# Six PSUM banks of scores: three sides of two banks in place of two sides of three

## The chip, the cores and the metric

The kernel runs on one core of a Trainium2 chip. A core has four engines that matter here: TensorE (PE in the profile) multiplies matrices and writes into PSUM, ScalarE (ACT) applies functions such as the exponential, VectorE (DVE) and GpSimd (POOL) do element-wise arithmetic. PSUM holds eight banks of 128 partitions x 512 float32 values; the kernel uses six of them for attention scores. The metric is the device time in microseconds. Before the change it was 778.63 us, the median of three runs (777.14 to 778.92).

## The reference: what is computed

```
g = sigmoid((x * gate_w).sum(-1))
q, k, v = split(x @ wqkv)                       # 32 heads of width 16, 2048 rows
a = softmax(q k^T / 4) v, joined over heads, @ wo
h = gelu(layernorm(x) @ w1); hs = shifted(h) @ w2; x1 = x + hs
b = x1 + gelu(layernorm(x1) @ w3) @ w4          # 512 -> 1792 -> 512
out = g * a + (1 - g) * b
```

The two halves read the same x (2048 x 512, bfloat16). The attention has 32 x 2048 x 2048 = 134 million scores, and each needs an exponential; that is most of the work outside TensorE.

## The kernel before

**Tiles.** The scores are made in blocks of 128 keys x 512 queries. A unit is four heads with one chunk of 512 queries; there are 32 units, each of 16 key tiles x 4 heads = 64 blocks, 2048 blocks in all. A score block (`score`, L749 to L756) is one matmul with only 32 rows of the array in use (a head's 16 values beside zeros), so blocks of different heads j lie in different row groups and run side by side.

**Two ways to the exponential.** Most blocks are read from PSUM by ScalarE, which writes the exponential as bfloat16 into a tile `pt` (`expo`, L1076). The others go to VectorE: it adds a constant and converts to int16 (`dump` in `whole`, L959), which gives the bits of a bfloat16 that is roughly the exponential. Four such blocks, one key tile for all four heads, make a quad; four further copies of the quad with other constants added (`shifted`, L1000 on VectorE, L998 on GpSimd) are made from it. TensorE sums all five copies in the product with v, and their errors cancel. So a block on ScalarE needs one product with v, and a block on VectorE needs five (`attend`, L1089).

**Slots and sides.** The first 34 slots (`EARLY`) have two banks each. After them six banks are used as two sides of three. Slot k uses side k % 2 (`stage`, L738 to L747). Either all three banks are ScalarE's and it reads 1536 elements per partition at once, or the slot also holds a block for VectorE (`dsc`; the rule WIDE is 1 in every unit), and ScalarE reads 1024 and VectorE 512. A slot of two kinds divides the side into two tiles, in a pool that is opened anew whenever the kind changes. The side is free again when both readers are done: `score_ready` (L716 to L736) waits for the exponential of slot k - 2 and for its dump. `lone_slot` gives a whole side to VectorE around the gelu stages.

**Order.** The order of all instructions is written out by a planner that runs while the kernel is built: four queues (pe, act, vector, pool) with estimated costs (MM, TURN, PE_OUT, ACT_OUT and the costs given to `post`), and it always takes the option that can begin first. TensorE's options are a score turn (`scores`), products with v (`attend`), steps of the projections (`job_run`), the last steps, and a `fill`, a multiplication by zero that keeps TensorE running. `wants_whole` decides whether a score turn carries blocks for VectorE: VectorE's queued work must be under DLIM, a room for the quad must be free, and fewer than CHAINS quads begun; it looks for a key tile that the unit hasn't reached, at most MAXD blocks to a unit. RULES holds such values for each of the 31 later units.

**Other work.** Projections and the MLP go through one more bank (`gen`), from which VectorE copies. The gelus sit in five places; each loads ScalarE's other table, applies the gelu in place to tiles that VectorE has copied, and then reads score sides that TensorE has filled with `g2T` or `hT` columns (`gelu_slot`, `expo_gelu`, L1053 and L1056): two slots of three tiles of 512 in each of the last four places. The last unit's last twelve blocks are cut into three ranges of queries (`split`, `end_slot`), so that the final sums can begin range by range.

Of the kernel before, what the change touches and what calls it, by code (L numbers as in the profile page):

```python
# [32 lines left out]
def kernel(  # L33
# [14 lines left out]
    P = 128  # L48
# [8 lines left out]
    PTB = 6  # L57
# [65 lines left out]
    idle = ptpool.tile([P, 3 * CH], BF16, tag="pt", name="idle")  # L123
# [39 lines left out]
    USUAL = {"WIDE": 1, "NEED": 36, "AHEAD": 8, "HURRY": 8, "DLIM": 0.9, "MANY": 2, "PTS": 4, "CHAINS": 4, "MAXD": 20}  # L163
    RULES = {1: {"MANY": 8, "NEED": 32, "WIDE": 1, "AHEAD": 16, "MAXD": 20, "PTS": 6, "CHAINS": 2, "HURRY": 14, "DLIM": 1.2}, 2: {"NEED": 24, "DLIM": 1.5, "HURRY": 24, "CHAINS": 2, "WIDE": 1, "PTS": 4, "AHEAD": 32, "MANY": 6, "MAXD": 16}, 3: {"WIDE": 1, "NEED": 30, "AHEAD": 20, "HURRY": 4, "DLIM": 1.2, "MANY": 8, "PTS": 5, "CHAINS": 4, "MAXD": 20}, 4: {"WIDE": 1, "NEED": 24, "AHEAD": 10, "HURRY": 0, "DLIM": 1.2, "MANY": 8, "PTS": 6, "CHAINS": 6, "MAXD": 20}, 5: {"WIDE": 1, "NEED": 22, "AHEAD": 16, "HURRY": 18, "DLIM": 2.1, "MANY": 8, "PTS": 6, "CHAINS": 3, "MAXD": 16}, 6: {"PTS": 4, "AHEAD": 6, "WIDE": 1, "DLIM": 2.5, "CHAINS": 3, "HURRY": 24, "MANY": 5, "MAXD": 16, "NEED": 34}, 7: {"WIDE": 1, "NEED": 36, "AHEAD": 24, "HURRY": 4, "DLIM": 1.8, "MANY": 6, "PTS": 5, "CHAINS": 4, "MAXD": 16}, 8: {"WIDE": 1, "NEED": 32, "AHEAD": 32, "HURRY": 14, "DLIM": 0.9, "MANY": 3, "PTS": 3, "CHAINS": 5, "MAXD": 12}, 9: {"DLIM": 1.2, "CHAINS": 2, "MANY": 2, "NEED": 26, "AHEAD": 4, "PTS": 4, "WIDE": 1, "HURRY": 4}, 10: {"MANY": 5, "PTS": 5, "HURRY": 24, "MAXD": 20, "AHEAD": 20, "CHAINS": 2, "NEED": 26, "DLIM": 0.9}, 11: {"WIDE": 1, "NEED": 40, "AHEAD": 8, "HURRY": 14, "DLIM": 1.2, "MANY": 5, "PTS": 6, "CHAINS": 3, "MAXD": 12}, 12: {"WIDE": 1, "NEED": 22, "AHEAD": 4, "HURRY": 24, "DLIM": 1.8, "MANY": 2, "PTS": 5, "CHAINS": 5, "MAXD": 16}, 13: {"WIDE": 1, "NEED": 26, "AHEAD": 12, "HURRY": 8, "DLIM": 0.9, "MANY": 6, "PTS": 6, "CHAINS": 6, "MAXD": 16}, 14: {"WIDE": 1, "CHAINS": 3, "HURRY": 8, "MANY": 6, "NEED": 40, "AHEAD": 32, "PTS": 3, "MAXD": 20, "DLIM": 1.8}, 15: {"DLIM": 2.1, "MAXD": 20, "PTS": 6, "CHAINS": 3, "NEED": 30, "HURRY": 24, "WIDE": 1, "MANY": 5, "AHEAD": 16}, 16: {"CHAINS": 3, "PTS": 4, "AHEAD": 16, "DLIM": 1.8, "HURRY": 4, "NEED": 36, "MANY": 4, "MAXD": 16}, 17: {"MAXD": 16, "DLIM": 0.9, "HURRY": 14, "NEED": 22, "PTS": 5, "WIDE": 1, "CHAINS": 2, "MANY": 4}, 18: {"NEED": 24, "AHEAD": 12, "MAXD": 16, "MANY": 5, "DLIM": 2.5, "CHAINS": 2, "HURRY": 4, "PTS": 6, "WIDE": 1}, 19: {"AHEAD": 8, "MAXD": 20, "DLIM": 1.2, "NEED": 26, "CHAINS": 6, "PTS": 3, "HURRY": 14, "MANY": 5}, 20: {"CHAINS": 2, "MAXD": 12, "WIDE": 1, "MANY": 4, "PTS": 3, "NEED": 30, "AHEAD": 20, "DLIM": 1.2, "HURRY": 24}, 21: {"MANY": 6, "NEED": 40, "CHAINS": 5, "WIDE": 1, "HURRY": 14, "DLIM": 2.1, "AHEAD": 12, "PTS": 3, "MAXD": 16}, 22: {"MANY": 5, "DLIM": 2.1, "AHEAD": 20, "WIDE": 1, "NEED": 40, "CHAINS": 4, "HURRY": 14, "PTS": 5, "MAXD": 16}, 23: {"MANY": 5, "NEED": 24, "DLIM": 2.1, "HURRY": 8, "AHEAD": 32, "WIDE": 1, "PTS": 6}, 24: {"MAXD": 16, "NEED": 28, "AHEAD": 16, "DLIM": 1.2, "MANY": 8, "PTS": 3, "WIDE": 1, "CHAINS": 3, "HURRY": 0}, 25: {"DLIM": 2.1, "PTS": 5, "NEED": 26, "WIDE": 1, "MAXD": 16, "HURRY": 14, "CHAINS": 2, "MANY": 5, "AHEAD": 8}, 26: {"WIDE": 1, "NEED": 28, "AHEAD": 10, "HURRY": 14, "DLIM": 1.8, "MANY": 3, "PTS": 3, "CHAINS": 5, "MAXD": 16}, 27: {"WIDE": 1, "NEED": 30, "AHEAD": 10, "HURRY": 0, "DLIM": 2.5, "MANY": 4, "PTS": 5, "CHAINS": 3, "MAXD": 12}, 28: {"NEED": 36, "PTS": 6, "WIDE": 1, "MAXD": 20, "DLIM": 1.8, "CHAINS": 5, "MANY": 4, "AHEAD": 6, "HURRY": 24}, 29: {"WIDE": 1, "NEED": 30, "AHEAD": 4, "HURRY": 24, "DLIM": 1.5, "MANY": 5, "PTS": 6, "CHAINS": 3, "MAXD": 16}, 30: {"WIDE": 1, "NEED": 26, "AHEAD": 24, "HURRY": 0, "DLIM": 1.5, "MANY": 4, "PTS": 5, "CHAINS": 2, "MAXD": 20}, 31: {"WIDE": 1, "NEED": 24, "AHEAD": 4, "HURRY": 24, "DLIM": 1.2, "MANY": 8, "PTS": 4, "CHAINS": 2, "MAXD": 12}}
    MM = 0.214
    TURN = 0.104
# [7 lines left out]
    VLIM = 2.0  # L174
    LASTNEED = 40
# [3 lines left out]
    LOOK = 0.1  # L179
# [3 lines left out]
    HOLD = (0.15, 0.5)  # L183
    MARGIN = 0.3
    CREDIT = 0.5
    LATER = 0.55
    GELU, WTWO = 1.0, 1.6
    MOST = 16.0
# [4 lines left out]
    SLACK = 0.25  # L193
# [4 lines left out]
    TANH = 3.0  # L198
    WINDOW = 3.4
    LOW = 0.45  # L200
    PINCH = 0.2
# [3 lines left out]
    state = {"n": 0, "gen": 0, "young": True, "mm": 0, "sp": 0.0, "before": True, "after": False, "aside": 0.0, "kind": "", "t": 0.0, "piece": 0.0,  # L205
# [273 lines left out]
    def mlp():  # L479
# [28 lines left out]
        for c in range(NC_):  # L508
            if c < NC_ - 1:
                norm(1, c + 1)  # L510
            g2T = pools["g"].tile([P, FT, CH], BF16, tag="g", name="g2T")
            for m in range(APART):
                yield from before_gelu(w3, m, res[0], g2T[:, m, :], ("z", c, m), all_at(("xnT", 1, c, KT - 1)))
            yield from gelu_all(("g", c), [g2T[:, m:m + 4, :] for m in range(0, APART, 4)],
                                all_at(*[("z", c, m) for m in range(APART)]), w3, res[0],
                                [(range(m, m + 3), g2T[:, m:m + 3, :]) for m in range(APART, FT, 3)])
            if c < NC_ - 1:
                res = []
                yield from norm_T(1, c + 1, res)
            for t in range(4 * c, 4 * c + 4):  # L520
                yield from w4_tile(g2T, w4, c, t)
# [133 lines left out]
    accs, stages, pts, old = {}, {}, {}, {}  # L655
    room = deque(epool.tile([P, 4, CH], I16, name=f"quad{i}")[:] for i in range(7))
    lone, undumped = set(), {}
    scored, dumped, done_exp, users, pt_free = {}, {}, {}, {}, {}
    banksets = [ExitStack(), ExitStack()]
    ctx.callback(lambda: [b.close() for b in banksets])  # L660
    kinds = [None, None]
    next_slot = {"score": 0, "exp": 0}
    group = {}

    def upcoming(count):
# [3 lines left out]
        while len(found) < count and n < len(units):  # L669
# [3 lines left out]
            if (m // 4, m % 4) not in taken[n]:  # L673
                found.append((n, m))
# [9 lines left out]
    def wants_whole(blocks, now, alone=0):  # L684
# [4 lines left out]
        most = alone or rule("WIDE")  # L689
        if quad["open"] is not None:  # L690
            n, kt, rest = quad["open"]
            most = min(most, len(rest))
            heads = [m % 4 for _, m in blocks[:3 - most]]
            fit = [j for j in rest if j not in heads]
            if len(fit) >= most or k - quad["last"] > 2 or alone:
                return n, kt, (fit + [j for j in rest if j in heads])[:most]
            return None
        heads = [m % 4 for _, m in blocks[:3 - most]]
# [17 lines left out]
    def score_ready(k):  # L716

        found = upcoming(1)
        if not found and not gelus and not ends:
            return None  # L720
        t = 0.0
        for n, m in () if gelus else upcoming(2 if k < EARLY else 3):
            c, u = units[n]
            for key in (("q", c, u // 2), ("k", u // 2, m // 4 * P // CH)):
                if key not in at:
                    return None
                t = max(t, at[key])
        if k >= 2:
            if k - 2 not in done_exp or dumped.get(k - 2, 0.0) is None:
                return None  # L730
            t = max(t, done_exp[k - 2] + 0.005, dumped.get(k - 2, 0.0) - 0.12)
        if k == EARLY:
            if k - 1 not in done_exp or banks[1] is None or banks[2] is None or state["bank"] and current["job"]:
                return None
            t = max(t, banks[1], banks[2])
        return t + 0.03  # L736

    def stage(k, kind):  # L738

        side = k % 2  # L740
        if kinds[side] != kind:
            banksets[side].close()
            kinds[side] = kind
            old[side] = banksets[side].enter_context(tc.tile_pool(
                name=f"psS{k}", bufs=1, space=bass.MemoryType.PSUM, side=("left", "right")[side], reuse_waits="tile"))
        st = old[side].tile([P, (3 - kind) * CH], F32, tag="stage", name="stage")
        return st, old[side].tile([P, kind * CH], F32, tag="dsc", name="dsc") if kind else None  # L747
# [10 lines left out]
    def gelu_slot(start):  # L758
        k = len(slots)
        item = turn[k] = gelus.popleft()  # L760
        _, _, _, w, rhs, ms, _, _ = item
        stages[k], _ = stage(k, 0)
        slots.append([])
        state["slot"] = len(slots)
        state["mm"] = 0
        for i, m in enumerate(ms):
            for kt in range(KT):
                strips(stages[k][:, i * CH:(i + 1) * CH], lhsT=w[:, kt, m * P:(m + 1) * P], rhs=rhs[:, kt, :],
                                 start=(kt == 0), stop=(kt == KT - 1))
        free["pe"] = start + (TURN if state["kind"] not in NARROW else 0.0) + len(ms) * KT * MM  # L770
        state["kind"] = "full"
        works(free["pe"] - len(ms) * KT * MM, free["pe"])
# [762 lines left out]
```

## Time and profile before

| | |
|---|---|
| median of three runs | 778.63 us |
| profiled execution | 777.81 us |
| its span, first to last instruction | 776.0 us |
| TensorE busy, share | 748.3 us, 96% |
| ScalarE busy, share | 759.2 us, 98% |
| VectorE busy, share | 717.1 us, 92% |
| GpSimd busy, share | 248.8 us, 32% |
| granted TensorE clock, mean | 1.000 |

A group's row gives its line, engine and operation, what is written from what, the shape, the count, then busy time and mean duration in ns, then the idle time of the engine just before these instructions and what ended it. Instructions of one engine overlap a little at their ends, so a mean duration is longer than the distance from one start to the next.

### The profile page before, as it was taken

What the parts mean: (1) busy time and instruction counts of PE and PEld (TensorE: products, weight loads), DVE (VectorE), ACT (ScalarE), POOL (GpSimd) and SP (SyncE); (2) the same over time, 40 slices, a digit from 0 to 9 for tenths busy, and PEclk for the clock granted to TensorE, in tenths of its full rate; (3) what the DMA queues carried; (4) which work ended last, traced back from release to release, by engine and by line L of the source; (5) the groups of instructions that cost most, each with busy time, mean ns of one, the idle gap of its engine ahead of it and who ended that gap; (6) DMA issues with size and microseconds to landing.
All of it is one profiled execution on the core that took longest, in us unless ns stands there. A gap on an engine that the chain in (4) does not pass through costs nothing.

```text
span 776.0 us, 23911 instructions
## 1 busy us (share of the span) xinstructions
PE 748.3 (96%) x10127; PEld 247.8 (32%) x10128; DVE 717.1 (92%) x1231; ACT 759.2 (98%) x730; POOL 248.8 (32%) x187
## 2 busy tenths in 40 slices
PE   8999999999999999899999999999999999999997
PEld 4334323333333233232223223323332223232233
DVE  5798999999999999999999999999998899989894
ACT  6999999999999999999999999999999999999996
POOL 3221433442313414234451334123224333311420
PEclk9999999999999999999999999999999999999999
DMA  9600012111130006002000013000020000000110
GB/s 198 199 24 18 16 47 64 33 32 42 18 37 19 19 18 125 20 16 46 20 17 22 20 33 45 17 11 14 19 53 21 16 19 26 20 29 6 33 32 31
DMA packets 52308, 29.05 MB, mean 37 GB/s; under 512 B 36713, under 2 KB 47721, under 8 KB 52201
## 3 DMA queue, kind: packets, MB, share of 16 engines
q1 hardware_dynamic: 51240, 27.00, 15.0%
q8 instruction: 79, 1.29, 0.7%
q10 hardware_dynamic: 960, 0.52, 0.2%
q14 instruction: 29, 0.23, 0.1%
HBM read 17.17 MB, written 2.35 MB: 25 GB/s over the span
## 4 chain that ended last, share of the span: by engine, by line
ACT 56%; PE 22%; issue 16%; DVE 5%; DMA 1%; POOL 1%; DVEq 0%; ACTq 0%; POOLq 0%; SPq 0%
ACT pt L1076 51%; PE acc L1089 8%; PE stage L754 7%; PE ps L271 2%; ACT g2T L1053 1%; PE ps_y L271 1%; DVE quad L959 1%; PE ps_o L271 1%; ACT g2T L1056 1%; DVE quad L1000 1%; ACT hT L1053 1%; DMA bcs<-rec_d 1%; POOL oT L1201 1%; ACT L1053 1%; PE warm L1335 0%
## 5 line engine op out<-in xcount | busy, mean ns | idle before, releaser
L1076 ACT ACTIVATE pt<-stage 128x1024 bf16<-128x1024 f32 (+1 forms) x686 | 709.3, 1220 | 4.5 <-PE dsc L754 2.1
L754 PE MATMUL stage<-qT,kT 32*128 32x512 bf16 (+1 forms) x1604 | 271.3, 379 | 18.0 <-ACT pt L1076 12.6
L959 DVE TENSOR_SCALAR quad<-dsc 128x512 int16<-128x512 f32 x346 | 230.6, 685 | 14.1 <-PE dsc L754 12.0
L998 POOL TENSOR_SCALAR quad<-quad 128x2048 int16<-128x2048 int16 x68 | 129.4, 1903 | 260.5 <-DVE quad L1000 146.4
L754 PE MATMUL dsc<-qT,kT 32*128 32x512 bf16 x468 | 179.9, 384 | 0.0
L754 PEld LDWEIGHTS <-kT 32*128 32x128 bf16 x2072 | 83.2, 91 | 284.0 <-issue 247.6
L1089 PE MATMUL acc<-pt,vp 128*17 128x512 bf16 (+3 forms) x1576 | 148.5, 379 | 2.5 <-DVE accsb L1171 1.8
L1000 DVE TENSOR_SCALAR quad<-quad 128x2048 int16<-128x2048 int16 x212 | 147.7, 710 | 1.3 <-PE acc L1089 1.2
L1089 PE MATMUL acc<-quad,vp 128*17 128x512 bf16 x1696 | 144.9, 381 | 0.1
L1089 PEld LDWEIGHTS <-vp 128*17 128x17 bf16 (+1 forms) x4056 | 83.1, 89 | 133.2 <-issue 97.2
L271 PE MATMUL ps<-w,g2T 128*32 128x512 bf16 x896 | 69.3, 382 | 0.0
L1201 POOL TENSOR_TENSOR oT<-accsb,bcs 128x512 bf16<-128x512 f32 x29 | 37.0, 1277 | 84.9 <-DVE quad L1000 60.1
L998 POOL TENSOR_SCALAR more<-more 128x2048 int16<-128x2048 int16 x17 | 32.3, 1897 | 80.8 <-DVE more L1000 33.1
L271 PE MATMUL ps_y<-xnT,w 128*32 128x512 bf16 x704 | 56.3, 383 | 1.0 <-DVE accsb L1171 0.8
L959 DVE TENSOR_SCALAR more<-dsc 128x512 int16<-128x512 f32 x69 | 45.9, 683 | 1.1 <-PE dsc L754 1.0
L998 POOL TENSOR_SCALAR xT<-xT 128x2048 int16<-128x2048 int16 x14 | 26.9, 1919 | 50.9 <-DVE quad L1000 44.4
L1089 PE MATMUL acc<-more,vp 128*17 128x512 bf16 x420 | 39.7, 380 | 0.0
L271 PEld LDWEIGHTS <-w 128*32 128x32 bf16 x1152 | 28.8, 95 | 33.0 <-issue 16.3
L959 DVE TENSOR_SCALAR xT<-dsc 128x512 int16<-128x512 f32 x53 | 35.2, 683 | 1.8 <-PE dsc L754 1.4
L1089 PE MATMUL acc<-xT,vp 128*17 128x512 bf16 x364 | 34.8, 381 | 0.0
L271 PE MATMUL acc<-wq,zero 128*32 128x512 bf16 x324 | 30.0, 383 | 0.0
L1000 DVE TENSOR_SCALAR more<-quad 128x2048 int16<-128x2048 int16 x39 | 27.8, 719 | 0.0
(120 smaller groups left out, 592.7 us busy)
## 6 DMA issues: line engine op xcount, KB each, us to landing
bcs<-rec_d SPq DMA_DIRECT2D x31, 256.0 KB
w<-in_B_w_dram SPq DMA_DIRECT2D x2, 1792.0 KB
out_dram<-ot SPq DMA_DIRECT2D x15, 128.0 KB
x_sb<-in_A_x_dram SPq DMA_DIRECT2D x14, 128.0 KB
oT<-oT SPq DMA_DIRECT2D x112, 16.0 KB
w<-in_B_w_dram SPq DMA_DIRECT2D x2, 512.0 KB
wkv<-in_A_wqkv_dram SPq DMA_DIRECT2D x1, 512.0 KB
wo_all<-in_A_wo_dram SPq DMA_DIRECT2D x8, 64.0 KB
```

The source lines that it names most:

```text
L271: nc.tensor.matmul(out[j:j + 32, :], lhsT=lhsT[:, j:j + 32], rhs=rhs, tile_position=(0, j), **kwargs)
L754: nc.tensor.matmul(out, lhsT=kT[G][32 * j:32 * j + 32, cc, o:o + P], rhs=qTs[(c, G)][32 * j:32 * j + 32, a, lo:hi], start=True, stop=True, ...
L959: nc.vector.tensor_scalar(out=bits[:, r:r + wide, :], in0=dsc.rearrange("p (a c) -> p a c", c=CH), scalar1=SHIFT, scalar2=LOWEST, op0=ALU. ...
L998: behind(nc.gpsimd.tensor_scalar(out=tiles[to], in0=tiles[base], scalar1=1.0, scalar2=shift, op0=ALU.mult, op1=ALU.add))
L1000: fast["ins"] = nc.vector.tensor_scalar(out=tiles[to], in0=tiles[base], scalar1=shift, scalar2=None, op0=ALU.add)
L1053: nc.scalar.activation(out=part, in_=part, func=ACT.Gelu_apprx_tanh)
L1056: nc.scalar.activation(out=dst, in_=stages.pop(k)[:, 0:len(ms) * CH].rearrange("p (a c) -> p a c", c=CH), func=ACT.Gelu_apprx_tanh)
L1076: nc.scalar.activation(out=pt[:, 0:w], in_=stages.pop(k)[:, 0:w], func=ACT.Exp, scale=LN2 / 128.0)
L1089: nc.tensor.matmul(accs[n][32 * j:32 * j + M, lo:hi], lhsT=lhsT, rhs=p, start=(kt == 0), stop=(kt == NT - 1), skip_group_check=True, tile_ ...
L1201: behind(nc.gpsimd.tensor_tensor(out=oT, in0=tiles["accsb"][:], in1=tiles["bcs"][:], op=ALU.mult))
```

## The change

The six banks become three pools of one tile each, two banks wide (`tri`), opened once. `sides` holds the time from which each is free, or None while it is used. ScalarE's slots always have two blocks, and VectorE's fetches always two blocks from a side of their own. `plan` decides when a score turn is made and for how many sides: if a second side will be free before ScalarE is due, the turn waits for both and fills two sides, four blocks, with two for ScalarE and either two for VectorE or two more for ScalarE; else it fills one. `order` lets the heads of a key tile be taken as 2, 3, 0, 1, so that the four blocks lie in four row groups. `alone` is a new TensorE option: a turn with two blocks for VectorE only, when VectorE has little queued. It takes the place of `lone_slot`.

Around it: `pt` tiles hold two blocks in place of three, and there are nine in place of six; the gelu slots take two tiles (three slots in each of the last four places instead of two); the last ranges are read in seven slots in place of four; the last step's PSUM tiles come from the same three sides; the planner's estimates MM and TURN are 0.002 lower; and RULES, USUAL and a dozen constants have new values. WIDE stays in the rules and isn't read any more. The core of the diff:

```diff
-    PTB = 6
+    PTB = 9
...
-                                [(range(m, m + 3), g2T[:, m:m + 3, :]) for m in range(APART, FT, 3)])
+                                [(range(m, m + 2), g2T[:, m:m + 2, :]) for m in range(APART, FT, 2)])
...
-        most = alone or rule("WIDE")
+        most = alone or 2
...
-        if k >= 2:
-            if k - 2 not in done_exp or dumped.get(k - 2, 0.0) is None:
-                return None
-            t = max(t, done_exp[k - 2] + 0.005, dumped.get(k - 2, 0.0) - 0.12)
...
+    def plan():
+
+        free_at = frees()
+        if gelus or ends:
+            return (free_at[0][0] + 0.03, 1, 0.0) if free_at else None
+        if not upcoming(1):
+            return None
+        t = keys_ready(2)
+        if t is None or not free_at:
+            return None
+        runs = [lasts(k) for k in pending()]
+        due_by = free["act"] + sum(runs) - ACT_OUT - TURN - 0.05
+        latest = due_by + PAIRW
+        first = max(t, free_at[0][0])
+        if len(free_at) > 1:
+            if max(t, free_at[1][0]) <= latest:
+                return max(t, free_at[1][0]) + 0.03, 2, due_by
+        elif runs and free["act"] + runs[0] + 0.115 <= latest:
+            return None
+        return first + 0.03, 1, due_by
...
+    def side_for(k):
+        side = frees()[0][1]
+        sides[side] = None
+        if k is not None:
+            side_of[k] = side
+        return side, tri[side].tile([P, 2 * CH], F32, tag="stage", name="stage")
...
+    def scores(start, count):
+        if gelus:
+            return gelu_slot(start)
+        if ends:
+            return end_slot(start)
+        begin = start + (TURN if state["kind"] != "score" else 0.0)
+        rows = [0, 0, 0, 0]
+        k = len(slots)
+        blocks = following_blocks()
...
+        mine = wants_whole(blocks, start) if count == 2 else None
+        put(side_for(k)[1], k, blocks, rows)
+        scored[k] = begin + (max(rows) - 1) * MM + ACT_OUT
+        if mine:
+            put_whole(mine, begin, rows)
+        elif count == 2 and not ends and (keys_ready(4) or 1e9) <= start:
+            blocks = following_blocks()
+            if blocks:
+                k = len(slots)
+                put(side_for(k)[1], k, blocks, rows)
+                scored[k] = begin + (max(rows) - 1) * MM + ACT_OUT
+        done_scores(begin, rows)
+
+    def put_whole(mine, begin, rows):
+        n, kt, js = mine
+        taken[n].update((kt, i) for i in range(4))
+        side, dsc = side_for(None)
+        for i, j in enumerate(js):
+            rows[j] += 1
+            score(dsc[:, i * CH:(i + 1) * CH], n, 4 * kt + j)
+        whole(side, dsc[:, 0:len(js) * CH], n, kt, js, begin + (max(rows) - 1) * MM + PE_OUT)
+
+    def alone_ready(f):
+
+        free_at = frees()
+        if state["young"] or state["ending"] or ends or not free_at:
+            return None
+        mlp = gelus or turn and max(turn) >= next_slot["exp"]
+        if not mlp and (len(pending()) < 2 or not SOLO) or gelus and len(free_at) < 2:
+            return None
+        t = max(f, free_at[0][0] + 0.03)
+        work = free["vector"] - t + sum(x[2] for x in queue["vector"] if not callable(x[4]) and x[4] < t + 1.0)
+        return t if work < (GLIM if mlp else SOLO) and wants_whole([], t, 2) else None
...
         def dump(end):
             nc.vector.tensor_scalar(out=bits[:, r:r + wide, :], in0=dsc.rearrange("p (a c) -> p a c", c=CH), scalar1=SHIFT, scalar2=LOWEST,
                                     op0=ALU.add, op1=ALU.max)
-            undumped[k] -= 1
-            if not undumped[k]:
-                dumped[k] = end
+            sides[k] = end - 0.12
...
-            pt = ptpool.tile([P, 3 * CH], BF16, tag="pt", name="pt")
+            pt = ptpool.tile([P, 2 * CH], BF16, tag="pt", name="pt")
...
         done_exp[k] = free["act"] + 0.11
+        if k in side_of:
+            sides[side_of[k]] = done_exp[k] + 0.005
```

More of the change, by code (lines that the diff above doesn't have):

```diff
@@ L167 @@
+    MM = 0.212
+    TURN = 0.102
     NARROW = ("full", "attend")
@@ L734, in score_ready, with frees, pending, lasts @@
                 return None
-            t = max(t, banks[1], banks[2])
+            t = max(t, banks[1], banks[2], done_exp[k - 1] + 0.005)
         return t + 0.03
[L738 to L747, printed above, removed]
+    def frees():
+        return sorted((t, s) for s, t in enumerate(sides) if t is not None)
+    def pending():
+        return range(next_slot["exp"], len(slots))
+    def lasts(k):
+        if k in turn:
+            return 0.05 + len(turn[k][5]) * CH / 1200 + sum(0.1 + p.free_size() / 1200 for p in turn[k][1])
+        return 0.051 + len(slots[k]) * cut.get(k, CH) / 1200
+    def plan():
+        free_at = frees()
+        if gelus or ends:
+            return (free_at[0][0] + 0.03, 1, 0.0) if free_at else None
+        if not upcoming(1):
+            return None
+        t = keys_ready(2)
+        if t is None or not free_at:
[10 more added lines that the diff above has]
+        return first + 0.03, 1, due_by
     def score(out, n, m, lo=0, hi=CH):
@@ L756, in score, with put @@
                          start=True, stop=True, tile_position=(32 * j, 0))
[L758 to L772, printed above, removed]
[L773 to L803 removed]
+    def put(st, k, blocks, rows):
         stages[k] = st
[L805 to L806 removed]
         for i, (n, m) in enumerate(blocks):
@@ new lines, in following_blocks, with gelu_slot @@
+    def following_blocks():
+        blocks = upcoming(2)
+        if place["n"] == len(units) - 1:
+            blocks = blocks[:max(0, remaining(place["n"]) - SPLIT - 4)]
+        return blocks
+    def side_for(k):
[4 more added lines that the diff above has]
+        return side, tri[side].tile([P, 2 * CH], F32, tag="stage", name="stage")
+    def gelu_slot(start):
+        k = len(slots)
+        item = turn[k] = gelus.popleft()
+        w, rhs, ms = item[3:6]
+        stages[k] = side_for(k)[1]
+        slots.append([])
+        state["slot"] = len(slots)
+        state["mm"] = 0
+        for i, m in enumerate(ms):
+            for kt in range(KT):
+                strips(stages[k][:, i * CH:(i + 1) * CH], lhsT=w[:, kt, m * P:(m + 1) * P], rhs=rhs[:, kt, :],
+                                 start=(kt == 0), stop=(kt == KT - 1))
+        free["pe"] = start + (TURN if state["kind"] not in NARROW else 0.0) + len(ms) * KT * MM
+        state["kind"] = "full"
+        works(free["pe"] - len(ms) * KT * MM, free["pe"])
+        scored[k] = free["pe"] - MM + ACT_OUT
```

231 lines of the change are left out of this document (100 added, 131 removed).

## The prediction

> **What bounds the kernel now.** I read the page first, then the table of windows, then ScalarE's groups by form, then the waits.
>
> ```profile
> span 776.0 us, 23911 instructions
> ...
> PE 748.3 (96%) x10127; PEld 247.8 (32%) x10128; DVE 717.1 (92%) x1231; ACT 759.2 (98%) x730; POOL 248.8 (32%) x187
> ...
> ACT 56%; PE 22%; issue 16%; DVE 5%; DMA 1%; POOL 1%; DVEq 0%; ACTq 0%; POOLq 0%; SPq 0%
> ...
> L1076 ACT ACTIVATE pt<-stage 128x1024 bf16<-128x1024 f32 (+1 forms) x686 | 709.3, 1220 | 4.5 <-PE dsc L754 2.1
> ...
> L271 PE MATMUL acc<-wq,zero 128*32 128x512 bf16 x324 | 30.0, 383 | 0.0
> ```
>
> ScalarE is busy 98% of the span and holds 56% of the chain that ended last. TensorE's 96% is softer: 30.0 us of it are multiplications by zero that the planner puts in to keep it running (the last row). By stage (the columns are the stretch, its length, then busy time and count of PE, PEld, DVE, ACT and POOL, the clock and the DMA):
>
> ```profile
> 0.00:40.00 40.00, 37.77 (x523) 15.97 (x527) 26.41 (x69) 33.68 (x38) 11.20 (x44) 1.00 0.79 195
> 40.00:740.00 700.00, 679.27 (x9192) 219.99 (x9196) 666.01 (x1122) 696.61 (x667) 230.67 (x139) 1.00 0.13 29
> 740.00:776.10 36.10, 31.23 (x420) 11.89 (x413) 24.65 (x42) 28.92 (x27) 6.96 (x4) 0.99 0.10 33
> ```
>
> From 40 to 740 us ScalarE lacks 3.4 us of 700. There is no idle time to win: only less work on ScalarE shortens this kernel, and that means handing score blocks to VectorE, which in the same stretch has 34.0 us idle (700 - 666.0). The start and the end are not touched by the change except in the order of the last slots. So the question is how much ScalarE's reads cost in their new size, and how many blocks VectorE can take over.
>
> **ScalarE: the price of a read.** The forms of its exponential, and a long run of each by the chain in order of time (start, length, what):
>
> ```profile
> L1076 ACT ACTIVATE pt<-stage 128x1024 bf16<-128x1024 f32 x504 | 477.3, 1106 | 4.0 <-PE dsc L754 2.1 <-PE stage L754 1.4
> L1076 ACT ACTIVATE pt<-stage 128x1536 bf16<-128x1536 f32 x181 | 255.1, 1539 | 0.5 <-PE stage L754 0.4
> ...
> L1076 ACT ACTIVATE pt<-stage 128x512 bf16<-128x512 f32 x1 | 0.9, 862 | 0.0
> ...
> 39.40 6.29 ACT pt L1076 x7
> ...
> 570.89 2.68 ACT g2T L1056 x2
> ```
>
> Seven reads of 1024 in 6.29 us are 0.90 us each; two of 1536 in 2.68 us are 1.34, nearer 1.33 since the second row's last read also shows its tail. I take 0.904 and 1.330: 0.426 for 512 elements, so 0.052 us of each read are fixed. At these prices the reads of before would be 504 x 0.904 + 181 x 1.330 + 0.5 = 696.8 us; the page has 709.3 busy and 4.5 idle, 713.8. The 17.0 us between are small waits, 25 ns on each of 686 reads.
>
> The change makes every read 1024. The elements are 504 x 1024 + 181 x 1536 + 512 = 794,624, or 776 reads instead of 686: 776 x 0.904 = 701.5, **+4.7 us**. The gelu slots go from three tiles to two, 12 of them in place of 8 in the last four stages: 4 x 0.052 = **+0.2**. The last ranges go from 4 reads to 7: 3 x 0.052, **+0.1**. Together +5.0 us before any block moves.
>
> [...]
>
> **VectorE: the price of fetching two.** All its fetches from the score banks (L959), all its shifts (L1000), and the shifts that GpSimd takes (L998), each as one row over the span, then single instructions with their starts:
>
> ```profile
> 0.00:776.10 776.10, 327.43 (x482) 1.00 0.16 37
> ...
> 0.00:776.10 776.10, 265.54 (x394) 1.00 0.16 37
> ...
> 0.00:776.10 776.10, 194.21 (x102) 1.00 0.16 37
> ...
> L959 DVE TENSOR_SCALAR quad<-dsc 128x512 int16<-128x512 f32 x346 | 230.6, 685 | 14.1 <-PE dsc L754 12.0
> ...
> L959 DVE TENSOR_SCALAR more<-dsc 128x512 int16<-128x512 f32 x69 | 45.9, 683 | 1.1 <-PE dsc L754 1.0
> ...
> L959 DVE TENSOR_SCALAR xT<-dsc 128x512 int16<-128x512 f32 x53 | 35.2, 683 | 1.8 <-PE dsc L754 1.4
> ...
> 223.14 0.68 DVE L959 TENSOR_SCALAR quad<-dsc 128x512 int16<-128x512 f32 x1
> 223.74 0.68 DVE L1000 TENSOR_SCALAR quad<-quad 128x2048 int16<-128x2048 int16 x1
> 224.34 1.40 DVE L959 TENSOR_SCALAR quad<-dsc 128x512 int16<-128x512 f32 x2
> ...
> 234.70 1.23 DVE L959 TENSOR_SCALAR quad<-stage 128x1024 int16<-128x1024 f32 x1
> 235.83 0.69 DVE L1000 TENSOR_SCALAR more<-more 128x2048 int16<-128x2048 int16 x1
> ```
>
> A chain handles four blocks (one quad) with four shifts. There are 394 + 102 = 496 shifts, so 124 quads or 496 blocks; 3.18 shifts of a quad run on VectorE and 0.82 on GpSimd. From start to start a fetch of one block takes 0.60 us (223.14 to 223.74), a shift 0.60 (223.74 to 224.34), a fetch of two 1.13 (234.70 to 235.83). 346 + 69 + 53 = 468 blocks are fetched singly; the 14 other fetches are already wider or alone. As 234 pairs they save 234 x 0.07 = **16.4 us** of VectorE. These single fetches also have 14.1 + 1.1 + 1.8 = 17.0 us of idle time ahead of them. Half as many fetches should halve it, **8.5 us**; bounds are nothing, if each pair waits twice as long because it needs two free sides, and 17.0.
>
> A quad more costs VectorE 2 x 1.13 + 3.18 x 0.60 = 4.2 us, and spares ScalarE two reads, 2 x 0.904 = 1.81 us. It costs TensorE 20 product blocks in place of 4, four groups of four strips more:
>
> ```profile
> 372.37 0.40 PE L1089 MATMUL acc<-pt,vp 128*32 128x512 bf16 x4
> 372.58 0.62 PE L1089 MATMUL acc<-quad,vp 128*17 128x512 bf16 x8
> ```
>
> Eight strips take 0.22 us more than four, so that is 0.9 us a quad, covered by the zero work above and by the score turns that fall away.
>
> How many quads? As the span shortens, VectorE's room shrinks with it: by 1.81 x 0.92 = 1.7 us a quad. The freed 24.9 us alone buy 24.9 / 5.9 = 4.2 quads. Then there are the 34.0 us idle between 40 and 740. The new `alone` turn gives VectorE a pair whenever its queue holds less than 0.6 us and a side is free, without waiting for ScalarE's next slot; I let a third of the 34.0, 11 us, be used: 1.9 more. I take **6 quads, -10.9 us** on ScalarE. Bounds: none (the chains are held back by rooms, CHAINS and NEED, which the change does not loosen in every unit), and 58.9 / 5.9 = 10 if all idle time goes.
>
> **TensorE and the third side.** The score turn of before writes three banks at most, 2072 blocks in somewhat over 686 turns. Four at once need at least 518, a pair at a time needs 1036; with some 260 VectorE pairs each joined to a ScalarE pair, and the rest half joined and half alone, about 640. At 0.22 that moves TensorE by some 10 us, off the path. Four row groups at once are in no row of before; I take them as concurrent like three, and the far end, a further 0.22 for each of 300 joint turns, 66 us, would eat the fillers and more.
>
> What matters is what waits. The joint turn waits for the later of two sides; behind it on TensorE stand the products (L1089) and projections (L271), for whose banks VectorE waits to evacuate. The waits of now:
>
> ```profile
> PE stage L754 <- ACT pt L1076: 12.6, 52, 0.8
> ...
> PEld L754 <- DVE quad L959: 13.8, 36, 0.5
> ...
> PEld L754 <- DVE more L959: 7.2, 16, 1.2
> ```
>
> Now a side comes free only when ScalarE's read and VectorE's fetch are both over, which is what the second and third rows show: 21.0 us in 52 waits. With three sides VectorE's fetch holds a side of its own, and ScalarE goes on between the other two. Against that, the 181 reads that gave TensorE 1.33 us to score the other side now give 0.90. I take the excess at 20 ns a read: 764 x 20 = 15.3 in place of 17.0, **-1.7 us**. Bounds: 10 ns (7.6 us, -9.4) and 45 ns (34.4, +17.4; those 52 waits' mean of 0.40 us on about every ninth read).
>
> **Sum.** 776.0 + 5.0 - 10.9 - 1.7 = 768.4 us of span. The profiled execution took 777.81 us, 1.8 more than its span, and lies 0.8 under the median of 778.63: 770.2, or 771.0 on the scale of the median. I say **771**, 1.0% faster. The nine narrower `pt` buffers hold the same 18 blocks as six wide ones and cost nothing.
>
> **Rivals.** First: *the freed VectorE time doesn't become quads*. For it: VectorE is already idle 34 us in the stretch where it could have worked, so something other than its time limits it there. Against: the idle time is split over 1122 instructions, 30 ns each. With one quad, and 2.6 from the span to the median's scale: 776.0 + 5.0 - 1.8 - 1.7 + 2.6 = 780, no change; 0.14.
>
> Second, on the other side: *ScalarE runs dry behind the short side*. While VectorE holds a side from its score to the end of a 1.13 us fetch, plus its queue, ScalarE lives on two sides of 0.90 us, each needing its own turn of TensorE in time; a turn that comes after a run of products is late. It decides from an excess of (17.0 + 5.9) / 764 = 30 ns a read, where the gain is gone. For it: the 1024 reads have 4.0 us idle before them and the 1536 only 0.5. Against: 0.80 us a time is the longest wait, and TensorE has turns to spare. At 40 ns: 776.0 + 5.0 - 10.9 + 13.6 + 2.6 = 786; 0.17.
>
> Third: *the third side frees both*. Ten quads and 15 ns: 776.0 + 5.0 - 18.1 - 17.0 + 11.3 + 2.6 = 760; 0.17. It needs VectorE full through the gelu stages too.
>
> Fourth: *a short read costs its whole fixed part*. By the mean durations, 1106 for 1024 and 1539 for 1536 ns, the fixed part would be 240 ns; 90 reads more would cost 21.7 in place of 4.7: 788. The row of seven reads speaks against it; 0.02. [...]
>
> My forecast has 0.50. A measurement of this kernel can tell 0.3% (2.3 us) from no change. Faster: 0.48 of mine and the third, 0.65. Same: most of the first, a little of mine and of the second, 0.15. Slower: most of the second, a third of the first and the fourth, 0.20. The range, 760 to 786, reaches from the third case to the second.
>
> **What would show it.** By form, ScalarE should have no 1536 exponential and about 764 of 1024 at 0.904 us; more than 770 says that quads were not won. VectorE's fetches should be some 260 of 128x1024, and shifts on both engines near 520. Exponentials' busy and idle time over their number, less 904 ns, gives the excess: over 30 ns is the second rival. Fewer than 2.5 blocks in a score turn, or zero work above 30 us gone to nothing, would show that TensorE became short. I am wrong in the main step if the number of shifts hardly moves.

## The result and the profile after

The changed kernel takes 785.03 us (median of four runs, 784.63 to 785.51) against 778.0: a ratio of 1.0092, 95% interval 1.008 to 1.0104. It is **slower by 0.9%**; forecast was 1.0% faster. The profiled execution took 785.16 us with a span of 783.4, 7.4 more than before.

From the page of the changed kernel, the rows that answer to those of before:

```profile
span 783.4 us, 23683 instructions
...
PE 763.3 (97%) x10048; PEld 249.8 (32%) x10048; DVE 726.3 (93%) x1021; ACT 764.5 (98%) x823; POOL 216.1 (28%) x169
...
PE 70%; ACT 19%; DVE 5%; issue 5%; POOL 0%; DVEq 0%; ACTq 0%; POOLq 0%
...
L1120 ACT ACTIVATE pt<-stage 128x1024 bf16<-128x1024 f32 x775 | 714.3, 1082 | 5.0 <-PE stage L785 4.0
```

All exponentials are reads of 1024 now, but for two of 512, and there are 775 of them, not 764. The nominal time is 773 x 0.904 + 2 x 0.478 = 699.7 us, 2.9 more than before's 696.8. Busy and idle time are 719.3, so 19.6 us of waits, 25 ns a read, where before had 17.0 and 24.8 ns. VectorE's fetches, VectorE's shifts and GpSimd's shifts, each as one row over the span:

```profile
0.00:784.00 784.00, 304.28 (x250) 1.00 0.16 37
...
0.00:840.00 840.00, 288.98 (x416) 1.00 0.14 35
...
0.00:840.00 840.00, 160.60 (x84) 1.00 0.14 35
```

250 fetches of two blocks are 125 quads: **one more than before, not six**. By these rows the fetches gave back 327.4 - 304.3 = 23.1 us of VectorE's time, and the shifts took 289.0 - 265.5 = 23.5. VectorE has 22 shifts more: 18 that GpSimd no longer does (102 to 84) and four for the added quad, 13 us at 0.60. The rest is shifts that last longer. In these rows instructions overlap at their ends; counted from each start to the next, the fetches take 18.6 us less and the shifts 25.9 more, and with 1.9 of other work VectorE is busier than before, 726.3 us against 717.1.

The idle time ahead of its fetches, which was to be halved to 8.5 us, is 14.6 + 2.4 + 3.2 = 20.2 us:

```profile
L1005 DVE TENSOR_SCALAR quad<-stage 128x1024 int16<-128x1024 f32 x176 | 214.3, 1217 | 14.6 <-PE stage L785 12.9
...
L1005 DVE TENSOR_SCALAR more<-stage 128x1024 int16<-128x1024 f32 x38 | 46.2, 1217 | 2.4 <-PE stage L785 2.1
L1005 DVE TENSOR_SCALAR xT<-stage 128x1024 int16<-128x1024 f32 x36 | 43.8, 1216 | 3.2 <-PE stage L785 2.9
```

### The profile page after: what moved, and what is told of

Read it like the earlier page. It is cut to its first block, busy times and chain, and to the rows that moved or that the text cites. A ratio compares the mean times of both kernels' runs of the same rounds, so it can differ in the third digit from the quotient of the medians.

```text
span 783.4 us, 23683 instructions
## 1 busy us (share of the span) xinstructions
PE 763.3 (97%) x10048; PEld 249.8 (32%) x10048; DVE 726.3 (93%) x1021; ACT 764.5 (98%) x823; POOL 216.1 (28%) x169
## 4 chain that ended last, share of the span: by engine, by line
PE 70%; ACT 19%; DVE 5%; issue 5%; POOL 0%; DVEq 0%; ACTq 0%; POOLq 0%
PE acc L1135 25%; PE stage L785 23%; ACT pt L1120 17%; PE ps L276 8%; PE ps_y L276 4%; PE stage L276 2%; PE ps_k L276 2%; PE ps_o L276 2%; PE ps_v L276 2%; DVE quad L1005 1%; PE ps_q L276 1%; DVE quad L1044 1%; ACT g2T L1095 1%; PE acc L276 1%; ACT g2T L1098 1%
## 5 line engine op out<-in xcount | busy, mean ns | idle before, releaser
L1120 ACT ACTIVATE pt<-stage 128x1024 bf16<-128x1024 f32 x775 | 714.3, 1082 | 5.0 <-PE stage L785 4.0
L785 PE MATMUL stage<-qT,kT 32*128 32x512 bf16 (+1 forms) x2072 | 294.7, 381 | 9.6 <-ACT pt L1120 7.5
L1005 DVE TENSOR_SCALAR quad<-stage 128x1024 int16<-128x1024 f32 x176 | 214.3, 1217 | 14.6 <-PE stage L785 12.9
L1044 DVE TENSOR_SCALAR quad<-quad 128x2048 int16<-128x2048 int16 x218 | 159.0, 745 | 1.2 <-PE acc L1135 0.8
L1135 PE MATMUL acc<-pt,vp 128*17 128x512 bf16 (+2 forms) x1572 | 146.6, 381 | 1.9 <-DVE accsb L1217 1.5
L1135 PE MATMUL acc<-quad,vp 128*17 128x512 bf16 x1712 | 144.7, 381 | 0.2 <-DVE quad L1044 0.2
L1135 PEld LDWEIGHTS <-vp 128*17 128x17 bf16 (+1 forms) x4072 | 84.5, 89 | 135.6 <-issue 100.4
L1005 DVE TENSOR_SCALAR more<-stage 128x1024 int16<-128x1024 f32 x38 | 46.2, 1217 | 2.4 <-PE stage L785 2.1
L1005 DVE TENSOR_SCALAR xT<-stage 128x1024 int16<-128x1024 f32 x36 | 43.8, 1216 | 3.2 <-PE stage L785 2.9
L1135 PE MATMUL acc<-more,vp 128*17 128x512 bf16 x412 | 40.0, 381 | 0.2 <-DVE more L1044 0.2
L276 PEld LDWEIGHTS <-w 128*32 128x32 bf16 x1152 | 28.9, 96 | 33.4 <-issue 18.9
L1135 PE MATMUL acc<-xT,vp 128*17 128x512 bf16 x376 | 36.1, 381 | 0.0
L1042 POOL TENSOR_SCALAR more<-more 128x2048 int16<-128x2048 int16 x10 | 19.0, 1901 | 51.8 <-DVE quad L1044 35.6
L276 PEld LDWEIGHTS <-g2T 128*32 128x32 bf16 x896 | 19.1, 95 | 23.8 <-issue 15.9
L1217 DVE COPY accsb<-acc 128x512 f32<-128x512 f32 x31 | 21.2, 683 | 4.6 <-POOL oT L1247 2.9
```

Source lines behind the costliest of these rows:

```text
L276: nc.tensor.matmul(out[j:j + 32, :], lhsT=lhsT[:, j:j + 32], rhs=rhs, tile_position=(0, j), **kwargs)
L785: nc.tensor.matmul(out, lhsT=kT[G][32 * j:32 * j + 32, cc, o:o + P], rhs=qTs[(c, G)][32 * j:32 * j + 32, a, lo:hi], start=True, stop=True, ...
L1005: nc.vector.tensor_scalar(out=bits[:, r:r + wide, :], in0=dsc.rearrange("p (a c) -> p a c", c=CH), scalar1=SHIFT, scalar2=LOWEST, op0=ALU. ...
L1042: behind(nc.gpsimd.tensor_scalar(out=tiles[to], in0=tiles[base], scalar1=1.0, scalar2=shift, op0=ALU.mult, op1=ALU.add))
L1044: fast["ins"] = nc.vector.tensor_scalar(out=tiles[to], in0=tiles[base], scalar1=shift, scalar2=None, op0=ALU.add)
L1120: nc.scalar.activation(out=pt[:, 0:w], in_=stages.pop(k)[:, 0:w], func=ACT.Exp, scale=LN2 / 128.0)
```

## The experiments

**One engine relieved, the plan kept.** The planner's order stays as it is; one engine's instructions cover fewer columns, and what they leave out is not computed. The engine is ScalarE (in the changed kernel and in the kernel before), TensorE, VectorE or GpSimd.

```diff
# act_trim and before_act_trim: expo
-        nc.scalar.activation(out=pt[:, 0:w], in_=stages.pop(k)[:, 0:w], ...)
+        read = w - 32 if trims(k) else w
+        nc.scalar.activation(out=pt[:, 0:read], in_=stages.pop(k)[:, 0:read], ...)
# pe_trim: w4_tile
+            wide = CH if m == 0 else CH // 2
-            bmm(ps[:], ..., rhs=w4[:, m, :],
+            bmm(ps[:, 0:wide], ..., rhs=w4[:, m, 0:wide],
# dve_trim: shifted, on VectorE
+                dst, src = (... [:, 0:4 * CH - (128 if n >= 6 else 0)] for x in (to, base))
# pool_trim: shifted, on GpSimd
+                dst, src = (... [:, 0:2 * CH if n >= 6 else 4 * CH] for x in (to, base))
```

> The changed kernel, its order of instructions kept to the last one; ScalarE's late exponentials read 992 of 1024 columns (the last 32 queries of the second block are left out of the output, and the products with v of that block are 480 wide), 0.027 us less on each of some 640 reads, 17 us of ScalarE and about 2 us of TensorE. If ScalarE alone sets the end, 785 falls to about 768. If TensorE sets it, as the chain of waits says with 70%, about 783. If the engines are bound together by the order, half: 774 to 779.

> The changed kernel, order kept; 13 of 14 steps of the last MLP product write 256 of 512 columns, so part of the output is left out: 208 groups of strips x 0.107 = 22 us less on TensorE. If TensorE sets the end, about 763 to 768. If ScalarE does, within 1 us of 785.

> The changed kernel, order kept; from unit 6 on VectorE's shifts cover 1920 of 2048 columns (the rest of each quad's terms is left as it lies): 0.033 us less on some 350 shifts, 11 us of VectorE. If VectorE's lateness sets the end, 774 to 778. If ScalarE or TensorE does, within 1.5 us of 785.

> The changed kernel, order kept; from unit 6 on GpSimd's shifts cover 1024 of 2048 columns (the other half is left as it lies), about 1.0 in place of 1.9 us each, 75 of them. VectorE's shifts that stand behind one of them lose most of their 22 us of extra length. If these collisions are why the time that VectorE won did no good, 779 to 782; if VectorE is not what sets the end, within 1.5 us of 785.

> The kernel before, its plan kept; ScalarE's late exponentials read 32 columns less each (the last 32 queries of each slot's last block are left out of the output): about 620 x 0.027 = 17 us less on ScalarE. The same trim gave the changed kernel 5.3 us. If the three sides tightened TensorE's supply of scores, the kernel before gains clearly more, 10 to 17 us: 761 to 768. If both are bound by TensorE just behind ScalarE, about 5: 772.

| run | ratio to the kernel before | against the changed kernel's 1.0092 |
|---|---|---|
| ScalarE, 660 reads 32 columns shorter, 17.8 us | 1.0026 (1.0016 to 1.0035) | 5 us less |
| TensorE, 22 us less by the plan (busy 763.3 to 754.8) | 1.0086 (1.0064 to 1.0109) | under 1 us, within 2 of none |
| VectorE, 11 us less by the plan (busy 726.3 to 716.9) | 1.0082 (1.0065 to 1.01) | under 1 us, within 2 of none |
| GpSimd's shifts halved | 1.0098 (1.0079 to 1.0116) | none, within 2 |
| kernel before, 566 reads 32 columns shorter, 15.3 us | 0.9915 (0.9899 to 0.9931) | 6.6 us less than itself |

Of the four, only ScalarE's time moves the end, and it gives a third of what it is relieved by. The chain of waits gave TensorE 70%, yet less of its work is worth nothing that can be told. The rest of ScalarE's relief turned into waits, as its reads show (the changed kernel with ScalarE trimmed; 113 reads of 1024 and two of 512 are in the row too):

```profile
L1121 ACT ACTIVATE pt<-stage 128x992 bf16<-128x992 f32 (+1 forms) x775 | 705.0, 1028 | 9.8 <-PE stage L785 6.3
```

At 0.904 - 0.027 = 0.877 us for the short reads, the 775 are 682.0; the row has 714.8, which is 42 ns a read in place of 25. The kernel before gains 6.6 us of 15.3, the changed kernel 5 of 17.8, so a tightening of TensorE's supply of scores, if there is one, is small. That GpSimd's halved shifts bring nothing, though VectorE's busy time falls from 726.3 to 715.0 us there, says that VectorE's lateness doesn't set this plan's end. With the order kept, these runs don't show what a new plan would make of the same relief.

**The price of a read.**

```diff
-        nc.scalar.activation(out=pt[:, 0:w], in_=stages.pop(k)[:, 0:w], ...)
+        for lo in range(0, w, 2 * CH):
+            hi = min(w, lo + 2 * CH)
+            nc.scalar.activation(out=pt[:, lo:hi], in_=st[:, lo:hi], ...)
```

> The kernel before, its plan kept, with each read of 1536 given as one of 1024 and one of 512: some 181 reads more at the 0.052 us worked out for the fixed part of a read, +9.4 us: 787. If a read's whole fixed part counted (0.24 us by the durations), 178 x 0.24 = 43 us more: 820. If the other engines had room beside ScalarE, within 2 us of 778.

788.49 us, ratio 1.0147 (1.0129 to 1.0165): 11.4 us for 181 reads (the page counts 911 instructions on ScalarE in place of 730: 686 reads have become 867), 63 ns each. The 0.052 us is right but for a little; the fourth rival's 240 ns is out.

**The two structures under one table.** RULES is emptied, so that all units go by USUAL. The values of USUAL differ in MANY and CHAINS (WIDE is 1 in the kernel before throughout), and each structure was run with both. The two still differ in the other constants of the change, so "structure" means the sides together with those.

```diff
-    RULES = {1: ..., 31: ...}
+    RULES = {}
# the second pair: USUAL of the other kernel (here the kernel before with the changed kernel's values)
-    USUAL = {..., "MANY": 2, ..., "CHAINS": 4, ...}
+    USUAL = {..., "MANY": 4, ..., "CHAINS": 6, ...}
```

> The kernel before with RULES empty, all units by its USUAL: both structures without the values of single units. It loses what the values won, some 20 to 35 us: 798 to 813.

> The changed kernel with RULES empty, all units by its USUAL. If the three sides themselves cost the 7 us, it lies 7 us or more above the kernel before without rules. If only the values of RULES are worse chosen than those of before, it lies level with it or below.

> The kernel before with RULES empty and the changed kernel's USUAL (MANY 4 and CHAINS 6 in place of 2 and 4, WIDE kept at 1): with the next run a second pair of the two structures under one table. If three sides are no worse, the pair lies within 1% like the first (817.6 and 813.8).

> The changed kernel with RULES empty and the kernel before's USUAL (MANY 2, CHAINS 4). Against the first run of the kernel before without rules (817.6, the same table): if three sides cost 7 us by themselves, 825; if not, level with it or below.

| USUAL | two sides of three | three sides of two |
|---|---|---|
| MANY 2, CHAINS 4 | 1.052 (1.0497 to 1.0543) | 1.0405 (1.0375 to 1.0435) |
| MANY 4, CHAINS 6 | 1.050 (1.0469 to 1.053) | 1.0471 (1.0449 to 1.0494) |

The kernel before loses 40 us without its rules, more than expected. Without rules for single units the three sides are faster by 1.1% in the first row; in the second the intervals touch. The exponential's group in these runs, in the order of the table's cells, row by row:

```profile
L1076 ACT ACTIVATE pt<-stage 128x1024 bf16<-128x1024 f32 (+1 forms) x686 | 723.6, 1241 | 17.5 <-PE acc L1089 8.7
```
```profile
L1120 ACT ACTIVATE pt<-stage 128x1024 bf16<-128x1024 f32 x793 | 730.1, 1088 | 4.8 <-PE stage L785 2.6
```
```profile
L1076 ACT ACTIVATE pt<-stage 128x1024 bf16<-128x1024 f32 (+1 forms) x685 | 714.1, 1232 | 30.2 <-PE acc L1089 27.0
```
```profile
L1120 ACT ACTIVATE pt<-stage 128x1024 bf16<-128x1024 f32 x793 | 731.1, 1096 | 6.5 <-PE stage L785 5.0
```

The first, 116 quads, is worth 710.5 us at the nominal prices, the second, 116 too, 716.0: 30.6 us of waits against 18.9. The third (121 quads, 701.9) and the fourth (116, 716.0) have 42.4 against 21.6. So the changed structure does take waits away, 12 and 21 us, and pays some 5 us for the added reads; what the narrower buffers and what the third side add to it was not told apart. It doesn't bring quads: 116 and 116 under the first table, 121 and 116 under the second. In the plans with rules for each unit, 17.0 us of waits were left to take.

**Both structures searched alike.** Unit after unit 100 random tables, twice over; the one whose plan ends first by the planner's estimate is kept. Same search and budget for both, each starting without rules from its own USUAL.

```diff
-    RULES = {...}      # the tables on record
+    RULES = {...}      # tables of this search
```

> The kernel before with RULES chosen anew: unit after unit, 100 random tables each, twice over, the one kept whose plan ends first by the planner's own estimate. The next run has tables from the same search with the same budget, so the two tell the structures apart when both are equally well searched. This one lies between its tables (777.5) and none (817): 785 to 795.

> The changed kernel with RULES from the same search. If its own tables are only worse searched than those of before, it keeps the 0.4 to 1.0% that it led by without tables, and lies 3 to 8 us below the run before it. If a good table wins less on three sides, since ScalarE's waits that a table can take away are already gone there, it lies level or up to 7 us above it.

Two sides: 786.65 us, ratio 1.0118 (1.0099 to 1.0138). Three sides: 791.71, 1.0179 (1.0162 to 1.0196), **0.6% slower**. The search won 31 us for the one (from 817.6) and 22 for the other (from 813.8). The number of quads is 120 and 119; the waits are 722.3 - 703.7 = 18.6 us and 725.4 - 710.6 = 14.8, from these groups (two sides, then three):

```profile
L1076 ACT ACTIVATE pt<-stage 128x1024 bf16<-128x1024 f32 (+1 forms) x687 | 715.9, 1226 | 6.4 <-PE acc L1089 2.7
```
```profile
L1120 ACT ACTIVATE pt<-stage 128x1024 bf16<-128x1024 f32 x787 | 723.2, 1096 | 2.2 <-PE stage L785 1.6
```

A searched table takes waits away in either structure. The reads cost 710.6 against 703.7 us, 6.9 more, 1.8 of them for the quad that is missing, less 3.8 of waits; that is 3.1 of the 4.7 us between the two spans (789.4 and 784.7). This is one search of each; its own scatter shows in the next two runs.

**What took VectorE's time.**

Both runs also have tables of their own from that search.

```diff
# after_pool_more
-    BACK = 0.6
+    BACK = 0.1
# after_pool_clear: shifted
-                post(..., 2.0 if to_pool else 0.69, ...)
+                post(..., 2.5 if to_pool else 0.69, ...)
```

> The changed kernel with BACK 0.1 in place of 0.6, so that a shift goes to GpSimd when VectorE has as little as 0.1 us queued, and RULES from the same search as the pair before: 86 shifts on GpSimd in the plan where that pair's changed kernel had 74. If shifts that came back to VectorE are what ate its 16 us, twelve of them are 7 us of VectorE: one or two quads more and 2 to 4 us less than 791.7. If not, within 1.5 us of it.

> The changed kernel with the planner's cost of a GpSimd shift 2.5 us in place of 2.0, so that VectorE's shifts are planned clear of it, and RULES from the same search. If VectorE standing behind GpSimd is what costs, its slow shifts fall from 33 to about 20 or fewer and the time lies 2 to 4 us below 791.7. If VectorE's lateness is no bound, the slow shifts fall and the time stays within 1.5 us or rises.

797.12 and 796.78 us, 5 us above the 791.7 they were to be compared with. Both tables come from a new search on a changed planner, and that alone may move 5 us, so as comparisons of time the two say nothing. The second did what was planned: 17 shifts of VectorE last over 0.76 us, 33 in the run it was to be compared with. What it still shows is in its windows:

```profile
40.00:740.00 700.00, 681.39 (x8978) 225.74 (x8977) 628.78 (x866) 694.48 (x746) 170.58 (x107) 0.99 0.13 28
```

VectorE is idle 71 us of 700 there, twice the 34 of the kernel before, and the trace has 403 + 73 = 476 shifts, 119 quads. In this plan, idle time of VectorE doesn't become quads.

**Quads forced.** DLIM is how much VectorE may have queued when a quad is begun. No rules for single units, USUAL's DLIM 0.9 raised:

```diff
-    USUAL = {..., "DLIM": 0.9, ...}
+    USUAL = {..., "DLIM": 1.1, ...}     # after_quads_some
+    USUAL = {..., "DLIM": 1.5, ...}     # after_quads_more
```

> The changed kernel without rules for single units, as in the first such run (813.8 us, 116 quads), but with DLIM 1.1 in place of 0.9, so that VectorE may have more queued when a quad is begun: 120 quads in the plan. If a quad more spares ScalarE 1.81 us and VectorE's idle time pays for it, 813.8 - 7 = 807. If VectorE's time is already used up where it counts, 812 or more.

> The same with DLIM 1.5: 130 quads in the plan. If quads pay, 14 x 1.81 = 25 us less than 813.8: 789. If VectorE then holds up the copies for TensorE and the scores for ScalarE, well above 813.8: 830 or more, with ScalarE's reads waiting far over 25 ns each.

116 quads took 813.8 us, 120 take 810.72, 130 take 838.74. The exponential's groups, 120 quads and then 130:

```profile
L1120 ACT ACTIVATE pt<-stage 128x1024 bf16<-128x1024 f32 x785 | 724.7, 1082 | 15.2 <-PE acc L1135 11.0
```
```profile
L1120 ACT ACTIVATE pt<-stage 128x1024 bf16<-128x1024 f32 x765 | 706.1, 1083 | 43.6 <-PE acc L1135 40.4
```

A quad spares ScalarE exactly two reads, as predicted: 793, 785, 765. But ScalarE begins to wait for products (L1135), 11.0 and then 40.4 us, where the run with 116 quads has no such row. All its waits at the exponentials rise from 21.6 us to 31.1 and 59.0, and so cost more than the 7.2 and 25.3 us of reads that are spared. The 3.1 us that 120 quads won are not theirs: ScalarE's last wait, at the end of the kernel, fell from 13.7 us to 1.3 in that plan (with 130 quads it is 23.2). One wait for a product, of 7.7 us, by the timeline of the run with 130 quads:

```profile
320.88 1.23 DVE L1005 TENSOR_SCALAR quad<-stage 128x1024 int16<-128x1024 f32 x1 [0.18 <-PE stage L785]
...
322.62 2.97 DVE L1044 TENSOR_SCALAR quad<-quad 128x2048 int16<-128x2048 int16 x3
322.73 1.70 POOL L1247 TENSOR_TENSOR oT<-accsb,bcs 128x512 bf16<-128x512 f32 x1 [1.72 <-issue]
...
325.75 1.90 POOL L1042 TENSOR_SCALAR quad<-quad 128x2048 int16<-128x2048 int16 x1 [1.31 <-DVE quad L1044]
...
327.96 0.40 PE L1135 MATMUL acc<-quad,vp 128*17 128x512 bf16 x4
...
328.29 0.40 PE L1135 MATMUL acc<-pt,vp 128*32 128x512 bf16 x4
...
328.78 1.02 ACT L1120 ACTIVATE pt<-stage 128x1024 bf16<-128x1024 f32 x1 [7.70 <-PE acc L1135]
```

The unit's last quad is fetched at 320.88. Its shifts follow one another on VectorE and GpSimd, and the last of its products goes out at 327.96. Only then does the next unit's first product (128*32, the first key tile) begin, since the kernel sums one unit at a time (`attend_option`); and only products free `pt` buffers. ScalarE, whose row names a product as what it waited for, stands from 321.08 to 328.78. In that stretch VectorE is busy 7.67 us of 7.70, in part with copies for the MLP, so here it is VectorE's time that is short, whatever is idle elsewhere:

```profile
321.08:328.78 7.70, 6.26 (x106) 2.77 (x106) 7.67 (x13) 0.00 (x1) 4.57 (x4) 1.00 0.06 18
```

## Why the prediction was wrong

**The sum.** The span was to be 768.4 us and is 783.4. Of these 15.0 us, 9.1 are quads that didn't come, 4.3 are waits, and 1.7 lie outside the terms of the sum. That 785 still falls into the stated range is luck: its upper end was worked out for the second rival, which did not come.

**Quads (-10.9 us, was -1.8).** This step failed. I took 24.9 us of VectorE's time as freed and a third of its idle time as usable, and spent both on quads at 4.2 us each: six. One came. Of the 24.9 us, the 8.5 of idle time ahead of the fetches was never freed (17.0 us became 20.2), and what the fetches gave back, the shifts took. Nor does time left over on VectorE make quads by itself: the plan with 71 us idle has 119. ScalarE's gain from a quad held (793 to 785 reads for four).

What stands against more quads is shown in the plans without rules. A quad's five terms must be summed before its unit closes, and a chain begun too late stops ScalarE, 40.4 us of it at 130 quads. The number there rises with DLIM (116, 120, 130 for 0.9, 1.1, 1.5), and the three sides don't raise it (116 and 116, 121 and 116). The plans with tables already have DLIM above 0.9 in many units: 7 to 11 of 31 where the tables were searched anew (119 and 120 quads), 27 and 25 of 31 with the tables on record (124 and 125). Which of the planner's conditions holds the number at 125 in the changed kernel as it was measured is not shown. The kernel before was not run with quads forced, either; without rules it waits 27.0 us for products at 121 quads where the changed kernel waits 11.0 at 120, so the three sides may well bear some more quads. The first rival had this outcome (one quad, 780), for a reason that I put no more exactly than "something other than its time limits it".

**Fetches of two (-16.4 us of VectorE).** Right: 1.13 us as read off the few wide fetches of before, and 23.1 us less busy time in the rows. It was taken up by shifts that GpSimd no longer got, and by those that stand behind GpSimd (29 that start within a GpSimd shift, against 24 before; 41 over 0.76 us, against 20). That this is the cause of the loss is not shown: with the order kept, relieving either engine changed nothing.

**Reads (+5.0 us).** Right; the split measured 63 ns in place of 52. With the one quad, the exponentials' reads cost 2.9 us more.

**Waits (-1.7 us, was +2.6).** The 21.0 us that TensorE waited for VectorE's fetches are gone (0.2 us is left), as the third side was to bring it. But ScalarE's waits did not shrink with them: they did without rules, by 12 and 21 us, and a searched plan has few left. Where the 2.6 us more come from is not shown; the idle time ahead of the exponentials grew from 4.5 to 5.0 us only. One stall has 2.2 of these 5.0. The timeline of the changed kernel, and its windows around it:

```profile
180.50 1.27 POOL L1247 TENSOR_TENSOR oT<-accsb,bcs 128x512 bf16<-128x512 f32 x1 [2.01 <-DVE quad L1044]
...
181.81 0.69 DVE L1217 COPY accsb<-acc 128x512 f32<-128x512 f32 x1 [1.44 <-POOL oT L1247]
...
182.55 0.40 PE L1135 MATMUL acc<-pt,vp 128*32 128x512 bf16 x4 [1.31 <-DVE accsb L1217]
...
183.60 0.61 PE L785 MATMUL stage<-qT,kT 32*128 32x512 bf16 x2
...
184.31 3.01 ACT L1120 ACTIVATE pt<-stage 128x1024 bf16<-128x1024 f32 x3 [1.68 <-PE stage L785]
```
```profile
180.00:183.00 3.00, 1.49 (x19) 0.52 (x18) 1.56 (x3) 2.63 (x3) 1.27 (x1) 0.99 0.00 0
183.00:187.00 4.00, 4.00 (x42) 1.03 (x38) 3.28 (x5) 2.64 (x3) 0.00 (x0) 0.58 0.08 18
```

GpSimd is late with a unit's scaling, VectorE waits 1.44 us for its buffer, TensorE 1.31 us for VectorE. After 3 us in which it was busy 1.49, TensorE's granted clock is 0.58 in the next 4; its matmuls take 0.61 us in place of 0.39, and ScalarE waits 1.68 us and once more 0.55. A like pause of the kernel before, 1.33 us before 725.72, in 3 us of which TensorE was busy 1.67 (723 to 726), left the clock at 1.00 (726 to 730). So of the 7.4 us, 2.9 are reads, 2.6 waits, 0.2 the gelu slots, and 1.7 were not followed; most of these lie at the two ends, where ScalarE is idle about 1.5 us longer than before.

**TensorE.** Four row groups at once are concurrent, as I took them: a turn of four takes 325 ns, one of three took 322. The score turns did not become 640 but 696 (686 before), most of them 320 of four blocks and 367 of two, counted as runs of that line's matmuls in the trace: while VectorE holds a side there is often no second one to fill. So TensorE was not relieved: its scores take 294.7 us in place of 273.4 by their rows, and its zero work fell from 30.0 to 22.6. That this cost time is not shown; relieving TensorE elsewhere, in the MLP, won nothing that can be told.

**The second rival** (ScalarE dry behind two sides, 40 ns a read) did not come: 25 ns.

**Structure or tables.** Under one USUAL the three sides are ahead by 1.1%, under the other not clearly, under tables searched alike they are behind by 0.6%, with the tables on record by 0.9%. Whether a longer search would close this is open; each search is one draw, and two more draws on a slightly changed planner lay 5 us off.

## What to carry to other kernels

Idle time of an engine, added up over the span, need not buy anything: ask by when each unit of the moved work must be done, and who stands still when it is late. Where an order is planned ahead, relieve one engine at a time with the order kept; here that took four runs, and told in which engine's time a saving is worth anything, while the chain of waits gave most to another. Compare structures under the same table before comparing them under their own, since here the tables alone move 29 to 41 us and the structure at most 9.

## What the runs showed of the hardware

In the traces of both kernels a VectorE shift that starts while GpSimd shifts does not end before GpSimd's. The changed kernel, VectorE and then GpSimd:

```profile
599.49 2.38 DVE L1044 TENSOR_SCALAR quad<-quad 128x2048 int16<-128x2048 int16 x1
```
```profile
599.12 2.21 POOL L1042 TENSOR_SCALAR quad<-quad 128x2048 int16<-128x2048 int16 x1 [3.93 <-DVE more L1044]
```

2.38 us in place of 0.68; GpSimd ends at 601.33, VectorE 0.54 us later. All 29 VectorE shifts that start within a GpSimd shift in this trace end 0.54 to 0.55 us after it, and all 24 of the kernel before 0.54 to 0.60. What holds VectorE in that time the traces don't show. The kernel before has 20 shifts longer than 0.76 us, the changed one 41, with halved GpSimd shifts 19.

A score turn of four row groups takes 325 ns from its first matmul to the next kind of work (median of 320 turns), one of three took 322 (median of 639), one of two 318 (median of 367).
